# Windowed attention with a feed-forward block: 256-token groups of all heads, a row maximum, and transposes by DMA

## The chip, the cores and the metric

The kernel runs on one core of a Trainium2 chip. A core has five engines, each with its own queue of instructions: PE (matrix multiplication), DVE (vector work), ACT (activation functions), POOL (general work, and the issue of transfers that cast) and SP (which here only issues transfers). Sixteen DMA engines move the data. The metric is the device time of one execution in microseconds.

## The reference

Four batches of eight heads, 768 tokens, 64 elements a head. Each query sees the 128 keys up to itself and the first four keys (the sinks). The heads are put side by side, 3072 tokens by 512, and go through a feed-forward block with a gate of the form h * sigmoid(1.702 h).

```python
scores = scale * np.matmul(q, k.transpose(0, 1, 3, 2))
keep = (pos[None, :] < n_sink) | ((rel >= 0) & (rel < window))
scores = np.where(keep, scores, -1000000000.0)
scores = scores - np.max(scores, axis=-1, keepdims=True)
a = np.exp(scores)
a = a / (np.sum(a, axis=-1, keepdims=True) + 1e-09)
x = np.matmul(a, v)                      # heads side by side: 3072 x 512
h = x @ w_in                             # 512 x 2048
out = (h * (1.0 / (1.0 + np.exp(-1.702 * h)))) @ w_out
```

## The kernel before

The attention works in 16 units of one batch and one pair of heads (768 tokens). For a unit, POOL issues loads that cast q, k and v from 32 to 16 bits straight into SBUF (`loads_qk`, `loads_v`, L129 to L143); each is cut into rows of 64 elements. `t_chunk` (L156 to L158) transposes q and k on PE against an identity matrix and DVE copies the result out of PSUM. `s_chunk` (L174) computes scores transposed, keys on the partitions and queries along the row, for the key blocks that a query can see; the first key block takes all 768 queries, for the sinks. ACT takes the exponential (L183), with no maximum subtracted, and `mask_chunk` multiplies two rows of 1920 columns by a 0/1 mask on DVE (L191). `av_chunk` (L207) multiplies with v, which carries a column of ones, so that the 65th column is the sum; DVE takes the reciprocal and normalises (L214, L215). `xt_chunk` (L227, L229) transposes the result on PE into xT.

The feed-forward block works in eight pieces of 384 tokens. `f_chunk` (L241) makes one of 16 hidden blocks: four matmuls, a tanh on ACT (L246), and a product on DVE (L247). `mm2_chunk` (L257) sums 16 matmuls into one bank of 128 tokens by 512, which ACT copies (L264) and SP stores (L265).

The loop over 16 units writes the order of PE's work out by hand: up to eight hidden blocks and two output blocks, taken from two lists as they become ready, stand between the score, transpose and value chunks of the neighbouring units. After the last unit, hidden and output blocks alternate. PSUM is shared out as four banks for scores and outputs, two for hidden blocks and two for transposes and values.

## Time and profile before

| | |
|---|---|
| runs, median (lowest to highest) | 262.49 us (261.63 to 263.02) |
| profiled execution, span from first to last instruction | 260.1 us |
| mean granted clock of PE | 0.998 |
| PE busy | 238.2 us |
| DVE busy | 158.6 us |
| ACT busy | 138.4 us |
| POOL busy | 74.3 us |
| DMA packets | 81607, 20.76 MB |
| of them in casting loads (q0) | 77696, 13.64 MB |
| HBM read, written | 27.79 MB, 6.29 MB |

The page gives the profiled execution by its span alone; the runs' times are taken around the whole launch. Busy shares are means over stages that differ: the first fifth of the span loads and computes attention, the middle mixes attention with the feed-forward block, the last quarter is feed-forward only. Idle time of an engine costs something only where another engine waits for it, so the rows that matter are those of the chain that ends last. PE's matmuls are pipelined: the distance between the starts of two is their price, not the duration of one.

### The profile page before, as it was taken

The numbers are of one execution on the slowest core, as the hardware profiler recorded it, in microseconds if no ns is written. First come the engines' busy times: TensorE is split into PE (matmuls) and PEld (weight loads), VectorE is DVE, ScalarE is ACT, GpSimd is POOL, SyncE is SP. The second block draws the span as 40 slices with busy tenths as digits, with TensorE's granted clock in tenths as the row PEclk, the third lists the DMA queues.
The fourth block names the chain that finished last, engine by engine and source line by source line (L and its number), as shares of the span: only waits on it lengthen the run. The fifth ranks groups of instructions, "written<-read, shape, count | busy, mean of one in ns | idle before, by whom it ended". The sixth has DMA issues, their size and how long they took to land.

```text
span 260.1 us, 4792 instructions
## 1 busy us (share of the span) xinstructions
PE 238.2 (92%) x1888; PEld 131.4 (51%) x1888; DVE 158.6 (61%) x320; ACT 138.4 (53%) x282; POOL 74.3 (29%) x92
## 2 busy tenths in 40 slices
PE   0749787999999999999999999999999999999993
PEld 0415444565646464555546464555545555555541
DVE  4337989898958685495918684493915833543300
ACT  1257666868438483757538483757533633644311
POOL 8977788773535151133310100000000000000000
PEclk9999999999999999999999999999999999999999
DMA  9999999999959393595960140101021011111112
GB/s 137 139 175 182 176 173 175 179 174 136 92 73 117 20 115 20 106 63 73 61 79 35 8 65 22 59 3 40 4 79 44 0 42 40 43 40 40 40 43 81
DMA packets 81607, 20.76 MB, mean 80 GB/s; under 512 B 75697, under 2 KB 78001, under 8 KB 81585
## 3 DMA queue, kind: packets, MB, share of 16 engines
q0 software_dynamic: 77696, 13.64, 66.1%
q1 hardware_dynamic: 3888, 6.82, 7.1%
q8 instruction: 15, 0.25, 0.4%
q14 instruction: 8, 0.06, 0.1%
HBM read 27.79 MB, written 6.29 MB: 131 GB/s over the span
## 4 chain that ended last, share of the span: by engine, by line
PE 82%; ACT 5%; DVE 4%; POOL 3%; DMA 3%; issue 1%; ACTq 0%; POOLq 0%
DMA qn_2_126<-in_q_dram 3%; PE o_1_2_3359 L257 1%; PE o_1_1_3339 L257 1%; PE o_1_0_3319 L257 1%; PE o_0_2_3267 L257 1%; PE o_0_1_3215 L257 1%; PE o_0_0_3163 L257 1%; PE o_1_2_3079 L257 1%; PE o_1_1_3027 L257 1%; PE o_1_0_2975 L257 1%; PE o_0_2_2809 L257 1%; PE o_0_1_2771 L257 1%; PE o_1_2_2584 L257 1%; PE o_1_1_2395 L257 1%; PE o_0_1_1985 L257 1%; PE o_0_0_1965 L257 1%
## 5 line engine op out<-in xcount | busy, mean ns | idle before, releaser
L241 PEld LDWEIGHTS <-w_in_77 128*128 128x128 f16 x512 | 47.8, 98 | 31.4 <-issue 1.1
L257 PEld LDWEIGHTS <-gT_1_90 128*128 128x128 f16 x48 | 4.7, 98 | 5.5
L257 PEld LDWEIGHTS <-gT_0_89 128*128 128x128 f16 x48 | 4.7, 98 | 5.3
L257 PEld LDWEIGHTS <-gT_0_87 128*128 128x128 f16 x48 | 4.7, 98 | 5.3
L257 PEld LDWEIGHTS <-gT_1_88 128*128 128x128 f16 x48 | 4.7, 98 | 5.3
L257 PEld LDWEIGHTS <-gT_1_84 128*128 128x128 f16 x48 | 4.7, 98 | 5.2
L257 PEld LDWEIGHTS <-gT_0_85 128*128 128x128 f16 x48 | 4.7, 98 | 5.2
L257 PEld LDWEIGHTS <-gT_1_86 128*128 128x128 f16 x48 | 4.7, 98 | 5.2
L156 PE MATMUL tqku_0_108<-ident_73,qn_0_91 128*128 128x128 f16 x2 | 0.6, 288 | 7.1 <-DMA qn_0_91<-in_q_dram 7.1
L257 PEld LDWEIGHTS <-gT_0_83 128*128 128x128 f16 x48 | 4.7, 98 | 4.8
L143 POOL DMA_DIRECT2D v_3_2433<-in_v_dram x1 | 1.0, 1007 | 15.3 <-issue 15.3
L183 ACT ACTIVATE ATu_136<-s0u_0_137 128x512 f16<-128x512 f32 x1 | 0.6, 597 | 7.9 <-PE s0u_1_138 L174 7.9
L156 PEld LDWEIGHTS <-qn_0_91 128*128 128x128 f16 x6 | 0.7, 125 | 7.1 <-issue 7.1
L247 DVE SCALAR_TENSOR_TENSOR gT_0_87<-th_0_6_2420,hT_0_6_2415 128x384 f16<-128x384 f16 x1 | 0.6, 553 | 5.9 <-ACT th_0_6_2420 L246 5.9
L257 PE MATMUL o_0_0_1145<-w_out_78,gT_0_83 128*128 128x512 f16 x16 | 4.1, 379 | 0.0
L247 DVE SCALAR_TENSOR_TENSOR gT_1_88<-th_1_6_2796,hT_1_6_2791 128x384 f16<-128x384 f16 x1 | 0.6, 554 | 5.7 <-ACT th_1_6_2796 L246 5.7
L247 DVE SCALAR_TENSOR_TENSOR gT_0_85<-th_0_6_1600,hT_0_6_1595 128x384 f16<-128x384 f16 x1 | 0.6, 553 | 5.3 <-ACT th_0_6_1600 L246 5.3
L247 DVE SCALAR_TENSOR_TENSOR gT_1_86<-th_1_6_2010,hT_1_6_2005 128x384 f16<-128x384 f16 x1 | 0.6, 553 | 5.3 <-ACT th_1_6_2010 L246 5.3
L257 PE MATMUL o_0_2_1360<-w_out_78,gT_0_83 128*128 128x512 f16 x16 | 3.8, 379 | 0.0
L257 PE MATMUL o_0_0_1965<-w_out_78,gT_0_85 128*128 128x512 f16 x16 | 3.8, 379 | 0.0
L257 PE MATMUL o_1_2_2584<-w_out_78,gT_1_86 128*128 128x512 f16 x16 | 3.8, 379 | 0.0
L257 PE MATMUL o_1_0_2375<-w_out_78,gT_1_86 128*128 128x512 f16 x16 | 3.8, 379 | 0.0
(1546 smaller groups left out, 810.9 us busy)
## 6 DMA issues: line engine op xcount, KB each, us to landing
w_in_77<-in_moe_w_in_dram POOLq DMA_DIRECT2D x4, 512.0 KB, 8.6
w_out_78<-in_moe_w_out_dram POOLq DMA_DIRECT2D x4, 512.0 KB, 8.8
maskall<-cmask SPq DMA_DIRECT2D x1, 480.0 KB, 3.9
out_dram<-osb_0_0_1146 SPq DMA_DIRECT2D x1, 256.0 KB, 2.1
out_dram<-osb_0_1_1166 SPq DMA_DIRECT2D x1, 256.0 KB, 3.6
out_dram<-osb_0_2_1361 SPq DMA_DIRECT2D x1, 256.0 KB, 3.6
out_dram<-osb_1_0_1556 SPq DMA_DIRECT2D x1, 256.0 KB, 3.7
out_dram<-osb_1_1_1576 SPq DMA_DIRECT2D x1, 256.0 KB, 2.3
```

What stands on the lines that cost most here:

```text
L143: nc.gpsimd.dma_start(v65[:, :, :, 0:D], v[b, h0 : h0 + 2].rearrange("h (i s) d -> s h i d", s=P))
L156: nc.tensor.transpose(tp[:, 0, i], qn[:, I], ident16)
L183: nc.scalar.activation(out=AT[:, hl, c0 : c0 + col], in_=st[hl][:, 0:col], func=AF.Exp, scale=scale,)
L241: nc.tensor.matmul(hT, w_in16[:, c, bass.ts(F, P)], xT[c][:, tok0 : tok0 + TT], start=(c == 0), stop=(c == 3),)
L247: nc.vector.scalar_tensor_tensor(out=gT[b, j][:, F], in0=th, scalar=1.0, in1=hT, op0=ALU.add, op1=ALU.mult)
L257: nc.tensor.matmul(ops, gT[b, j][:, F, bass.ts(t4, P)], w_out16[:, F], start=(F == 0), stop=(F == NF - 1),)
```

## The change

The kernel is written anew around groups of 256 tokens of one batch and all eight heads; there are 12. The order of every engine is the order of the program text.

- q and k are cast into DRAM (`load_qk`) and come from there transposed by DMA (`transposed_qk`). The exponentials, the sink weights and the normalised result are transposed by DMA from SBUF to SBUF (L238, L250, L300). All transposes are issued by SP.
- Scores have queries on the partitions. A query block sees its own key block and the one before; of the two, each column is needed from exactly one, so a predicated copy on DVE puts both into one tile of 128 columns (`maxima`). DVE then takes the row maximum, and its minimum form with the sinks' becomes the bias of the exponential (`weights`). After the transpose, the tile is parted again: a select on POOL (`up`) and a mask product on DVE (`lo`) (`parts`).
- Sinks are computed apart (`sinks`, `sink_weights`), as 64 columns for all heads, and enter the value product through a table `vs` of their values.
- The hidden block covers 256 tokens, two blocks to a bank, and the gate is one activation from PSUM to the 16-bit gT (`hidden`). `out_part` makes an output block in four parts; ACT copies and stores it.
- Iteration n of the loop holds the attention of group n, the hidden blocks of group n - 1 and the output blocks of group n - 2. The first two score tiles of group n + 1 are made at its end.
- PSUM: two score tiles of two banks each, two hidden banks, one value bank (shared with the sinks), one output bank.

```diff
+TG = 256
+BIG = 1.0e9
+def _take_prev(first: bool) -> np.ndarray:
+    q, c = np.arange(P)[:, None], np.arange(P)[None, :]
+    m = np.broadcast_to((c > q)[:, None, None, :], (P, 2, 2, P)).copy()
+    if first:
+        m[:, :, 0] = ((c > q) & (c >= 4))[:, None]
+    return m.astype(np.uint16).reshape(P, 4 * P)
+def _own(first: bool) -> np.ndarray:
+    c, q = np.arange(P)[:, None], np.arange(P)[None, :]
+    m = np.broadcast_to((c <= q)[:, None, None, :], (P, 2, 2, P)).copy()
+    if first:
+        m[:, :, 0] = True
+    return m.astype(np.float16).reshape(P, 4 * P)
+def _sink_off(n_sink: int) -> np.ndarray:
+    q, j = np.arange(P)[:, None], np.arange(n_sink)[None, :]
+    m = np.zeros((P, 4, 2, 2, n_sink), np.float32)
+    m[:, :, 0] = BIG
+    m[:, :, 1] = np.where(q >= j, 0.0, BIG)[:, None, None, :]
+    return m.reshape(P, 16 * n_sink)
...
+    ctx.enter_context(tc.manual_schedule())
...
+    q16 = [[dram.tile([TG, DM], FP16, name=f"q16_{b}_{t}") for t in range(NT)] for b in range(B)]
+    k16 = [[dram.tile([TG, DM], FP16, name=f"k16_{b}_{t}") for t in range(NT)] for b in range(B)]
...
+    def load_qk(g: int):
+        b, t = divmod(g, NT)
+        for src, dst in ((q, q16), (k, k16)):
+            nc.gpsimd.dma_start(
+                dst[b][t].rearrange("s (h d) -> s h d", h=H),
+                src[b, :, bass.ts(t, TG)].rearrange("h s d -> s h d"),
+            )
...
-    def t_chunk(u: int):
...
-    def s_chunk(u: int, part: int):
...
-    def mask_chunk(u: int):
...
-    def av_chunk(u: int, g: int):
...
-    def xt_chunk(u: int, g: int):
...
-    def f_chunk(b: int, j: int, F: int, nth: int):
...
-    def mm2_chunk(b: int, j: int, t4: int, nsplit: int = 1):
...
+    def transposed_qk(g: int):
+        b, t = divmod(g, NT)
+        if t == 0:
+            KT[b] = work.tile([P, HP, S], FP16, tag="kT", bufs=2, name=f"kT{b}")
+        nc.sync.dma_start_transpose(KT[b][:, :, bass.ts(t, TG)], k16[b][t])
+        qT = work.tile([P, HP, TG], FP16, tag="qT", bufs=3, name=f"qT{g}")
+        nc.sync.dma_start_transpose(qT, q16[b][t])
+        G[g]["qT"] = qT
+    def sink_keys(b: int):
+        for h in range(2):
+            nc.gpsimd.tensor_copy(
+                out=kd[b][bass.ts(h, D), :, bass.ts(h, n_sink)],
+                in_=KT[b][bass.ts(h, D), :, 0:n_sink],
+            )
...
+    def sinks(g: int):
+        b, t = divmod(g, NT)
+        qT = G[g]["qT"]
+        sk = psp.tile([P, HP, 2, 2 * n_sink], FP32, tag="av", bufs=1, name=f"sk{g}")
+        for hp in range(HP):
+            for i in range(2):
+                nc.tensor.matmul(sk[:, hp, i], qT[:, hp, bass.ts(i, P)], kd[b][:, hp], start=True, stop=True)
+        sn = work.tile([P, 16, n_sink], FP32, tag="sn", name=f"sn{g}")
...
+            nc.vector.tensor_scalar(out=flat, in0=skf, scalar1=-scale, scalar2=None, op0=ALU.mult)
+        m2 = work.tile([P, 16], FP32, tag="m2", name=f"m2{g}")
+        nc.vector.tensor_reduce(out=m2, in_=sn, axis=AX.X, op=ALU.min)
+        G[g].update(sn=sn, m2=m2, bias=work.tile([P, 16], FP32, tag="bias", name=f"bias{g}"))
+    def scores(g: int, hp: int):
+        b, t = divmod(g, NT)
+        qT, kT = G[g]["qT"], KT[b]
+        nat = psp.tile([P, 2, 2, 2 * P], FP32, tag="nat", bufs=2, name=f"nat{g}_{hp}")
+        for i in range(2):
+            I = 2 * t + i
+            if I == 0:
+                for h in range(2):
+                    r = bass.ts(h, D)
+                    nc.tensor.matmul(nat[:, h, i, 0:P], masked_l[r], masked_r[r], start=True, stop=True)
+            for h in range(2):
+                r = bass.ts(h, D)
+                lo = max(I - 1, 0) * P
+                o = nat[:, h, i, P:] if I == 0 else nat[:, h, i]
+                nc.tensor.matmul(
+                    o, qT[r, hp, bass.ts(i, P)], kT[r, hp, lo : (I + 1) * P], start=True, stop=True
+                )
+        G[g]["nat", hp] = nat
+    def maxima(g: int, hp: int):
+        t = g % NT
+        natf = G[g]["nat", hp].rearrange("p h i c -> p (h i) c")
+        nc.vector.copy_predicated(
+            out=natf[:, :, P:], mask=take_prev[t == 0].rearrange("p (a c) -> p a c", a=4), data=natf[:, :, 0:P]
+        )
+        m1 = work.tile([P, 2, 2], FP32, tag="m1", name=f"m1{g}_{hp}")
+        nc.vector.tensor_reduce(
+            out=m1.rearrange("p h i -> p (h i)"), in_=natf[:, :, P:], axis=AX.X, op=ALU.max
+        )
+        nc.vector.scalar_tensor_tensor(
+            out=G[g]["bias"][:, bass.ts(hp, 4)].rearrange("p (i h) -> p i h", i=2),
+            in0=m1.rearrange("p h i -> p i h"),
+            scalar=-scale,
+            in1=G[g]["m2"][:, bass.ts(hp, 4)].rearrange("p (i h) -> p i h", i=2),
+            op0=ALU.mult,
+            op1=ALU.min,
+        )
+    def weights(g: int, hp: int):
+        nat, bias = G[g]["nat", hp], G[g]["bias"]
+        A = work.tile([P, 4, P], FP16, tag="A", bufs=3, name=f"A{g}_{hp}")
+        for h in range(2):
+            for i in range(2):
+                c = 4 * hp + 2 * i + h
+                nc.scalar.activation(
+                    out=A[:, 2 * h + i], in_=nat[:, h, i, P:], func=AF.Exp, bias=bias[:, c : c + 1], scale=scale
+                )
+        AT = work.tile([P, 4, P], FP16, tag="AT", bufs=4, name=f"AT{g}_{hp}")
+        nc.sync.dma_start_transpose(AT, A.rearrange("p a c -> p (a c)"))
+        G[g]["AT", hp] = AT
+    def sink_weights(g: int):
+        sn, bias = G[g]["sn"], G[g]["bias"]
+        ts_ = work.tile([P, 16, n_sink], FP32, tag="ts", name=f"ts{g}")
+        nc.vector.tensor_tensor(
+            out=ts_, in0=bias.unsqueeze(2).broadcast_to((P, 16, n_sink)), in1=sn, op=ALU.subtract
+        )
+        As = sinkA[g % 2]
+        nc.scalar.activation(out=As[:, 0:64], in_=ts_.rearrange("p a j -> p (a j)"), func=AF.Exp)
+        AsT = work.tile([P, 1, P], FP16, tag="AsT", bufs=2, name=f"AsT{g}")
+        nc.sync.dma_start_transpose(AsT, As)
+        G[g]["AsT"] = AsT
+    def parts(g: int, hp: int):
+        t = g % NT
+        AT = G[g]["AT", hp]
+        lo = work.tile([P, 4, P], FP16, tag="lo", bufs=3, name=f"lo{g}_{hp}")
+        up = work.tile([P, 4, P], FP16, tag="up", bufs=3, name=f"up{g}_{hp}")
+        nc.gpsimd.affine_select(
+            out=up, in_=AT, pattern=[[0, 4], [-1, P]], compare_op=ALU.is_gt, fill=zero_reg, base=0,
+            channel_multiplier=1,
+        )
+        nc.vector.tensor_tensor(
+            out=lo.rearrange("p a c -> p (a c)"), in0=AT.rearrange("p a c -> p (a c)"), in1=own[t == 0], op=ALU.mult
+        )
+        G[g]["lo", hp], G[g]["up", hp] = lo, up
+    def values(g: int, hp: int):
+        b, t = divmod(g, NT)
+        lo, up, AsT = G[g]["lo", hp], G[g]["up", hp], G[g]["AsT"]
+        av = psp.tile([P, 2, 2, D + 1], FP32, tag="av", bufs=1, name=f"av{g}_{hp}")
+        for i in range(2):
+            I = 2 * t + i
+            if I > 0:
+                nc.tensor.matmul(
+                    av[:, i].rearrange("p h d -> p (h d)"), AsT[:, 0],
+                    vs[b][:, 4 * hp + 2 * i : 4 * hp + 2 * i + 2].rearrange("p h d -> p (h d)"),
+                    start=True, stop=False,
+                )
+            for h in range(2):
+                head = 2 * hp + h
+                if I > 0:
+                    J = I - 1
+                    nc.tensor.matmul(
+                        av[:, i, h], up[:, 2 * h + i], vn[b][J // 2][:, J % 2, head], start=False, stop=False
+                    )
+                nc.tensor.matmul(
+                    av[:, i, h], lo[:, 2 * h + i], vn[b][t][:, i, head], start=(I == 0), stop=(I == 0 or h == 1)
+                )
+        if hp == 0:
+            G[g]["xn"] = work.tile([P, 2, HP, 2, D], FP16, tag="xn", name=f"xn{g}")
+        rcp = work.tile([P, 2, 2], FP32, tag="rcp", name=f"rcp{g}_{hp}")
+        nc.vector.reciprocal(out=rcp, in_=av[:, :, :, D])
+        nc.vector.tensor_tensor(
+            out=G[g]["xn"][:, :, hp], in0=av[:, :, :, 0:D], in1=rcp.to_broadcast((P, 2, 2, D)), op=ALU.mult
+        )
+    def x_transposed(g: int):
+        xT = work.tile([P, 2 * HP, P], FP16, tag="xT", bufs=3, name=f"xT{g}")
+        nc.sync.dma_start_transpose(xT, G[g]["xn"].rearrange("p i a h d -> p (i a h d)"))
+        G[g]["xT"] = xT.rearrange("p (i c) s -> p i c s", i=2)
+    def hidden(g: int, F2: int):
+        xT = G[g]["xT"]
+        if F2 == 0:
+            G[g]["gT"] = work.tile([P, NF, TG], FP16, tag="gT", name=f"gT{g}")
+        hT = psp.tile([P, 2, 2, P], FP32, tag="hT", bufs=2, name=f"hT{g}_{F2}")
+        for f in range(2):
+            F = 2 * F2 + f
+            for c in range(4):
+                nc.tensor.matmul(
+                    hT[:, f], w_in16[:, c, bass.ts(F, P)], xT[:, :, c], start=(c == 0), stop=(c == 3)
+                )
+        nc.scalar.activation(
+            out=G[g]["gT"][:, 2 * F2 : 2 * F2 + 2].rearrange("p f s -> p (f s)"),
+            in_=hT.rearrange("p f i s -> p (f i s)"),
+            func=AF.Gelu_apprx_sigmoid,
+        )
+    def out_part(g: int, i: int, part: int):
+        b, t = divmod(g, NT)
+        if part == 0:
+            G[g]["o", i] = psp.tile([P, DM], FP32, tag="o", bufs=1, name=f"o{g}_{i}")
+        o, gT = G[g]["o", i], G[g]["gT"]
+        for F in range(4 * part, 4 * part + 4):
+            nc.tensor.matmul(o, gT[:, F, bass.ts(i, P)], w_out16[:, F], start=(F == 0), stop=(F == NF - 1))
+        if part == 3:
+            osb = work.tile([P, DM], FP32, tag="osb", bufs=3, name=f"osb{g}_{i}")
+            nc.scalar.copy(osb, o)
+            r = b * S + t * TG + i * P
+            nc.scalar.dma_start(out[r : r + P, :], osb)
...
+    transposed_qk(0)
+    sink_keys(0)
+    load_v(1)
+    load_w_in(1)
+    load_w_in(2)
+    load_w_in(3)
+    sink_values(0)
+    load_qk(2)
+    load_v(2)
+    load_w_out(0)
+    load_w_out(1)
+    load_w_out(2)
+    load_w_out(3)
+    def ahead(n: int):
+        if n < NG:
+            sinks(n)
+            for hp in (0, 1):
+                scores(n, hp)
+                maxima(n, hp)
+    ahead(0)
+    for n in range(NG + 2):
+        att = n < NG
+        g1, g2 = n - 1, n - 2
+        if n + 1 < NG:
+            transposed_qk(n + 1)
+            if (n + 1) % NT == 0:
+                sink_keys((n + 1) // NT)
+        if att:
+            weights(n, 0)
+        if 0 <= g2:
+            out_part(g2, 0, 0)
+            out_part(g2, 0, 1)
+        if att:
+            weights(n, 1)
+            scores(n, 2)
+            maxima(n, 2)
+            weights(n, 2)
+        if 0 <= g2:
+            out_part(g2, 0, 2)
+            out_part(g2, 0, 3)
+        if att:
+            scores(n, 3)
+            maxima(n, 3)
+        if 0 <= g2:
+            out_part(g2, 1, 0)
+        if att:
+            weights(n, 3)
+            sink_weights(n)
+            parts(n, 0)
+        if 0 <= g2:
+            out_part(g2, 1, 1)
+            out_part(g2, 1, 2)
+            out_part(g2, 1, 3)
+        if n + 3 < NG:
+            load_qk(n + 3)
+            load_v(n + 3)
+        if n + 1 < NG and (n + 1) % NT == 0:
+            sink_values((n + 1) // NT)
+        if n == 0:
+            ahead(1)
+        f1 = 0 <= g1 < NG
+        for F2 in range(NF // 2):
+            if f1:
+                hidden(g1, F2)
+            if att and F2 in (0, 1, 2):
+                parts(n, F2 + 1)
+            if att and F2 in (2, 3, 4, 5):
+                values(n, F2 - 2)
+            if F2 == 5 and n > 0:
+                if n + 1 < NG:
+                    sinks(n + 1)
+                    scores(n + 1, 0)
+                    maxima(n + 1, 0)
+            if F2 == 6 and n > 0 and n + 1 < NG:
+                scores(n + 1, 1)
+                maxima(n + 1, 1)
+        if att:
+            x_transposed(n)
```

## The prediction

> **What bounds the kernel now.** I read the page's busy shares and slices first, then the chain in order of time, then stretches, then single rows for prices.
>
> ```profile
> span 260.1 us, 4792 instructions
> PE 238.2 (92%) x1888; PEld 131.4 (51%) x1888; DVE 158.6 (61%) x320; ACT 138.4 (53%) x282; POOL 74.3 (29%) x92
> PE   0749787999999999999999999999999999999993
> ACT  1257666868438483757538483757533633644311
> DMA  9999999999959393595960140101021011111112
> ```
>
> PE is full from slice 8 on; the DMA engines are full only before that. The chain says the same: loads in the first 20 us, then PE line after PE line to the end.
>
> ```profile
> 11.02 7.15 DMA qn_2_126<-in_q_dram
> ...
> 80.90 0.66 PE avu_1_1279 L207 x18
> 81.56 0.65 PE hT_1_8_1302 L241 x4
> 82.21 0.17 PE xtu_0_1310 L227 x3
> ...
> 93.69 0.10 PE s3u_0_1466 L174
> ...
> 102.23 3.45 PE o_1_1_1575 L257 x16
> 249.29 3.45 PE o_1_1_3339 L257 x16
> ```
>
> Seen here: 0.163 us a hidden matmul of 384 columns, 0.216 an output matmul of 512, 0.037 a value matmul of 65, 0.055 a 128-column transpose, and 0.11 a pair of 256-column scores (0.10 here, s3u_1 runs beside s3u_0). The stretches show where PE waits and where not:
>
> ```profile
> 0.00:47.00 47.00, 30.56 (x326) 18.39 (x327) 31.60 (x63) 24.84 (x50) 38.94 (x51) 1.00 1.76 166
> 75.00:190.00 115.00, 113.90 (x927) 62.34 (x926) 75.86 (x155) 68.36 (x140) 19.79 (x23) 1.00 0.48 53
> ```
>
> Columns: length, PE, weight loads, DVE, ACT, POOL, granted clock (1.00), DMA share, GB/s. ACT has 47 us of slack in the second stretch, so ACT's waits cost nothing now.
>
> Prices for the other engines, from the timeline and the DMA issues:
>
> ```profile
> 0.73 1.28 ACT L183 ACT_TABLE_LOAD   x1 [0.73 <-PEq L368]
> 7.77 0.27 PE L157 MATMUL tqku_0_108<-ident_73,kn_0_92 128*128 128x128 f16 x1 [0.26 <-DMA kn_0_92<-in_k_dram]
> 20.22 0.59 POOL L103 DMA_DIRECT2D w_in_77<-in_moe_w_in_dram  x1
> 26.50 0.59 POOL L103 DMA_DIRECT2D w_in_77<-in_moe_w_in_dram  x1
> 102.89 0.33 SPq L265 DMA_DIRECT2D out_dram<-osb_1_0_1556  x1
> 108.01 0.42 DVE L158 COPY qkTu_1637<-tqku_0_1638 128x512 f16<-128x512 f16 x1
> 109.86 0.20 DVE L214 RECIPROCAL rcpu_0_1658<-avu_0_1656 128x6 f32<-128x6 f32 x1 [0.27 <-PE avu_0_1656 L207]
> 110.09 0.56 DVE L215 TENSOR_TENSOR xnu_0_1657<-avu_0_1656,rcpu_0_1658 128x384 f16<-128x384 f32 x1
> 110.68 0.59 ACT L183 ACTIVATE ATu_1622<-s3u_1_1682 128x512 f16<-128x512 f32 x1
> 256.29 0.66 ACT L264 ACTIVATE osb_1_2_3360<-o_1_2_3359 128x256 f32<-128x256 f32 x2 [2.91 <-PE o_1_2_3359 L257]
> ...
> out_dram<-osb_0_0_2752 SPq DMA_DIRECT2D x1, 256.0 KB, 2.0
> qn_3_636<-in_q_dram POOLq DMA_DIRECT2D x2, 96.0 KB, 7.8
> ```
>
> **The change: PE work.** Before: 512 x 0.163 + 384 x 0.216 = 166 us, plus per head pair 12 x 0.055 + 0.82 (3840 score columns, two heads side by side, at 0.11 per 512) + 30 x 0.037 + 6 x 0.055 = 2.9, x16 = 47; 213 in all. After: hidden 768 x 0.109 (two thirds of 0.163) = 84, output 83, and per group scores 4 x 0.22, sinks 8 x 0.037, values 4 x 0.41 = 2.8, x12 = 34; 200. The transposes leave PE: 13 us less. One full iteration is 6.9 output + 7.0 hidden + 2.8 = 16.7 us.
>
> **Where it waits.** Ten iterations (n = 2 to 11) are full. The program now has 21 table loads on the way, 27 us at 1.28, since Exp and the gate alternate; it had one. I walk one iteration from the moment PE ends the last hidden pair. ACT's prices: 128 columns cost 0.19 each in a row (the eight ACTIVATEs of a unit, 3840 columns, run from 107.40 to 111.27, 0.84 ns a column) to 0.27 alone (0.59 less 384 x 0.84 ns); I take 0.25, as a per-partition bias has no row, so 1.05 for the four of a head pair. The gate and a copy, both 128x512: 0.6. DVE: 0.20 fixed and 0.96 ns a column (0.56 at 384) give 0.70 for 512; predicated copy 0.70, maximum 0.70, small row 0.20 = 1.65 for one `maxima` with handovers. Both large ones have no row: 0.42 (the plain copy) to 0.75; I take 0.70, nearest to two-operand work on PSUM.
>
> - ACT: last gate to 0.65, table load to 1.95, weights 0 to 3.0, weights 1 to 4.05. PE: output parts to 1.72, then `scores(n,2)` needs the bank that weights 0 frees: 1.4 us idle, done at 3.3; parts to 5.0, `scores(n,3)` to 5.25.
> - DVE: maxima 2 to 5.05; ACT: weights 2 to 6.15, copy of the output bank to 6.75. That bank exists once, so the second output block starts at 6.85: 1.6 us idle; PE ends it at 10.3. Weights 3 and sink weights finish at 8.4 beside it.
> - ACT: copy to 10.95, the store's issue 0.33 (it moves from SP to ACT, so the table load queues behind it), table load to 12.6, gate to 13.2. PE has two hidden banks, so the third pair waits from 12.05 to 13.25: 1.2 us. Then hidden and values to 18.4; `sinks(n+1)` shares the one value bank and waits 0.7 for DVE; end 21.6.
>
> So 16.7 + 4.9 = 21.6 us. With the short prices (exponentials 0.19, DVE 0.42) the same walk gives 20. DVE's other work (lo 4 x 0.34, normalisation 4 x 0.65) totals 11 us and lies beside PE.
>
> The Trainium skill, "ScalarE: Activation LUTs", What ACT_TABLE_LOAD costs, states about 2.66 us for a switch including a drain, and its rule to batch calls by table set speaks against this change. The trace's one load took 1.28, at a moment with nothing to drain. By the page's figure both loads on the way grow by 1.4 and the walk gives 24.4 (an estimate), 28 us more in all.
>
> **Transposes by DMA.** No row. Below: the 256 KB store, 2.0 us to landing; above: a load of 768 short rows on full queues, 7.8. I take 3.5, nearer the store, which like these is one SP issue. At 3.5 the weights of the last head pair (8.15) and the sinks are in by 12.4, before values at 14.1: hidden. At 7.8 they come at about 16.3, and an iteration is 2.2 longer. The last transpose of an iteration (x) is issued at about 19 and needed 10 us into the next one. SP is one queue: the k and q transposes of group n+1 wait there for their loads, and behind them stand all weight transposes of group n. If those loads were late, values, normalisation and the next hidden block would be late by the same amount; their cover is that loads run three groups ahead.
>
> **Loads.** Steps of 6.28 us (20.22 to 26.50) carried 4608 rows and a 512 KB weight part. A group of 6144 rows is therefore at most 8.4 us; two thirds of the rows now go to DRAM and back, unpriced: from no more to double, 14 us. Either is under 20 and hidden once started. POOL's queue counts too: each group's four issues (about 1.2 + 1.2 + 0.9 + 0.9, from 0.82 for 768 rows and 1.03 for 1536) stand between its first and second select. A select has no POOL row; 0.3 (mask multiply rate) to 1.0 (its longest issue), I take 1.0; covered.
>
> **The start.** q and k of group 0: the first 3072 rows were in at 7.77; 4096 rows, about 9.5. Transposes 13, scores 15, weights of group 0 from 15.6 to 21.9. POOL copies the sink keys at 13.5, when kT is there, and behind them issues v (2 x 0.9), three w_in (0.6), the sink values (no row, taken as 2), q and k (2 x 1.2), v, four w_out (0.8): 26.5. After the first select, group 3's four loads wait for group 2's to land (bytes at the rate of the 6.28 us steps: about 29) and end at 31.8; three more selects 34.8. So values of group 0 end at 36 and x is transposed at 39.5, where the first hidden block begins. Iteration 1's second select stands behind loads that wait for w_out, in at about 40; with 7.0 of hidden and 1.6 of values between, it ends at 50. Bounds: 42 if POOL is never late, 63 if three transposes in series take 7.8. PE had done 30.6 us of work by 47 before; here it will have done about 12.
>
> **The end.** Iteration 12: output 6.9 + 0.7, hidden 7.0; then gate 0.65, output 7.6, copy and store 3: 26.
>
> **Sum.** 50 + 10 x 21.6 + 26 = 292 us of span. The page gives the profiled execution's span, 260.1; the runs (261.63 to 263.02, median 262.49) stand 1.5 to 2.9 above it. I add 2.4 for what lies around the span, as the median does: 294.
>
> **Rivals.** (a) Faster: PE stays the bound because ACT's table loads fall under output matmuls. Speaking for it: 13 us less PE work, 47 us of ACT slack in a 115 us stretch. Against: the single output bank and the two score banks tie PE to ACT's order. At 17.5 an iteration and a start of 45: 45 + 175 + 26 + 2.4 = 248. It decides below 18.4 an iteration (at a start of 50). (b) Slow transposes: 7.8 us each, 63 + 10 x 23.8 + 26 + 2.4 = 329; DMA at 0.48 share in the steady stretch speaks against queues being that full. (c) The loads through DRAM double: the start grows by about 5 and nothing else, 299; inside the forecast's range.
>
> **How the numbers follow.** Forecast with (c), 272 to 315: 0.60. Rival (a), under 261.2: 0.12. Within 0.5% of 262.5 (about what a measurement tells from no change): 0.03. Between that and 272: 0.05. Rival (b), 315 to 338: 0.13; beyond, if transposes and loads are slow together: 0.07. The range 260 to 338 leaves out most of (a) and the last 0.07. The forecast's own range is 272 to 315.
>
> **What would show it.** PE's busy share near 70%, ACT_TABLE_LOAD x22; PE idle before L203 on ACT L234 (1.4), before L328 on ACT L331 (1.6), before L312 on ACT L315 (1.2); iterations about 21.6 apart by the stores; transposes landing in 3 to 4 us. Wrong if iterations are under 18.4, or if PE waits on DMA for AT or kT in the steady part.

## The result and the profile after

The changed kernel takes 377.96 us in the median (374.37 to 380.04, four runs) against 262.51 us for the kernel before in the same session: a ratio of 1.432, 95% interval 1.422 to 1.442. The ratio leaves out the execution of 380.04 us, which was in the chip's slower state; the two medians by themselves give 1.440. The forecast was 294.0 us with a range of 260 to 338. The direction was right, the size was not. The profiled execution has a span of 372.2 us and took 374.37 us.

The page of the changed kernel, busy shares and slices:

```profile
span 372.2 us, 5170 instructions
PE 229.4 (62%) x1904; PEld 145.7 (39%) x1904; DVE 140.1 (38%) x352; ACT 152.7 (41%) x346; POOL 100.7 (27%) x120
PE   0010211367767767667667677587587877878995
...
PEclk9999999999989989989989989989989999999999
DMA  9997999995987975945927955924915163321101
```

No engine is full. PE has little to do before 74 us. From there to about 280 us PE stays near 0.7, DMA comes in bursts near 0.9, and PEclk loses a tenth once in about three slices, which is once an iteration. Only at the end, when no loads are left, PE rises to 0.8.

An iteration can be cut at ACT's table load for Exp. These come at 89.38, 116.65, 143.28, 171.02, 198.64, 225.28, 252.59, 280.27, 302.70 and 325.59 us. The first seven distances, during which the loads of later groups run, have a mean of 27.27 us; the last two are 22.43 and 22.89 us. Two stretches of the changed kernel, cut in this way (columns: length, busy time with counts for PE, weight loads, DVE, ACT, POOL, then granted clock, DMA share, GB/s), one with loads and one without. The DMA share of a stretch sums the times of all packets that start in it over 16 engines, and as packets overlap it can pass 1.

```profile
198.64:225.28 26.64, 18.80 (x154) 11.97 (x152) 10.99 (x28) 12.90 (x29) 7.18 (x8) 0.94 1.00 96
...
302.70:325.59 22.89, 17.92 (x162) 11.26 (x160) 10.69 (x28) 12.90 (x29) 2.94 (x4) 1.00 0.44 74
```

ACT does the same 12.90 us in both. What differs is the DMA share, 1.00 against 0.44, and the granted clock, 0.94 against 1.00.

PE's rows of the first of these iterations, in order of time (A holds the exponentials, AT their transpose, AsT that of the sink weights); the bracket is the idle time before a row and what ended it:

```profile
201.13 0.23 PE L198 MATMUL nat<-maskedr,maskedl 64*128 64x128 f16 x2 [1.40 <-ACT A L234]
...
205.00 3.61 PE L328 MATMUL o<-w_out,gT 128*128 128x512 f16 x16 [1.32 <-ACT osb L331]
...
211.58 1.03 PE L312 MATMUL hT<-xT,w_in 128*128 128x256 f16 x8 [1.22 <-ACT gT L315]
...
215.75 0.29 PE L275 MATMUL av<-vs,AsT 128*128 128x130 f16 x1 [3.07 <-DMA AsT<-sinkA]
...
216.07 1.90 PE L312 MATMUL hT<-xT,w_in 128*128 128x256 f16 x8
...
218.21 1.26 PE L312 MATMUL hT<-xT,w_in 128*128 128x256 f16 x8
...
221.69 0.34 PE L175 MATMUL sk<-kd,qT 128*128 128x8 f16 x8 [0.83 <-DVE xn L294]
```

And of the one without loads:

```profile
309.06 3.61 PE L328 MATMUL o<-w_out,gT 128*128 128x512 f16 x16 [1.32 <-ACT osb L331]
...
315.64 1.03 PE L312 MATMUL hT<-xT,w_in 128*128 128x256 f16 x8 [1.22 <-ACT gT L315]
316.51 0.22 PE L275 MATMUL av<-vs,AsT 128*128 128x130 f16 x1
```

The waits for ACT and DVE (1.40, 1.32, 1.22, 0.83 us) are the same in both; the prediction's walk had 1.4, 1.6, 1.2 and 0.7. New is the fourth row of the first fence: 3.07 us for the transposed sink weights AsT. The rows behind it are slower as well: eight hidden matmuls take 1.90 and 1.26 us where 1.03 is usual. Wait and slower matmuls together are 4.2 us. That is the whole difference between this iteration, 26.64 us, and the one without loads that also holds the first group of a batch, 22.43 us (280.27 to 302.70). Over the seven iterations PE waits 22.9 us for AsT, 3.3 us each.

Why AsT is late can be read from the two queues that issue transfers. SP in the same iteration:

```profile
201.14 6.86 SPq L238 DMA_TRANSPOSE AT<-A  x4
208.10 1.18 SPq L250 DMA_TRANSPOSE AsT<-sinkA  x1
```

and POOL:

```profile
203.58 0.63 POOL L259 TENSOR_SCALAR_AFFINE_SELECT up<-AT 128x512 f16<-128x512 f16 x1 [13.16 <-DMA AT<-A]
204.16 1.23 POOL L114 DMA_DIRECT2D q<-in_q_dram  x1
205.26 1.40 POOL L114 DMA_DIRECT2D k<-in_k_dram  x1
206.28 2.14 POOL L122 DMA_DIRECT2D vn<-in_v_dram  x2
```

The first weight transpose is issued at 201.14 and its reader starts at 203.58: at most 2.44 us to landing. Behind that reader POOL issues the four loads of group n + 3. AsT, issued at 208.10 into those loads, is used at 215.75: 7.65 us, and 7.6 to 8.1 in all seven. In the three iterations without loads it was in use 4.3 to 4.4 us after its issue, with no wait for it.

The start, from PE's rows:

```profile
20.18 0.37 PE L175 MATMUL sk<-kd,qT 128*128 128x8 f16 x8 [20.18 <-DMA qT<-q]
...
36.48 0.29 PE L198 MATMUL nat<-maskedr,maskedl 64*128 64x128 f16 x2 [14.96 <-ACT A L234]
...
50.80 0.29 PE L275 MATMUL av<-vs,AsT 128*128 128x130 f16 x1 [8.25 <-DMA AsT<-sinkA]
...
65.93 3.57 PE L312 MATMUL hT<-xT,w_in 128*128 128x256 f16 x16 [8.15 <-DMA xT<-xn]
75.07 1.86 PE L312 MATMUL hT<-xT,w_in 128*128 128x256 f16 x8 [5.57 <-ACT gT L315]
```

and ACT's:

```profile
3.64 31.55 ACTq L349 DMA_DIRECT2D vsr<-in_v_dram  x16
35.29 2.18 ACT L234 ACTIVATE A<-nat,bias 128x128 f16<-128x128 f32 x8 [30.40 <-DMA vsr<-in_v_dram]
```

Sixteen small loads of the sinks' values, issued by ACT, keep ACT's queue from 3.64 to 35.2 us, so that the first exponentials come at 35.3 us; then the transposes of the sink weights and of x take 7.8 and 8.4 us each from issue to use, one after the other. Iteration 2 starts at 89.4 us.

### The profile page after: what moved, and what is told of

Read it like the earlier page. It is cut to its first block, busy times and chain, and to the rows that moved or that the text cites. A ratio compares the mean times of both kernels' runs of the same rounds, so it can differ in the third digit from the quotient of the medians.

```text
span 372.2 us, 5170 instructions
## 1 busy us (share of the span) xinstructions
PE 229.4 (62%) x1904; PEld 145.7 (39%) x1904; DVE 140.1 (38%) x352; ACT 152.7 (41%) x346; POOL 100.7 (27%) x120
## 3 DMA queue, kind: packets, MB, share of 16 engines
q0 software_dynamic: 78720, 13.64, 48.7%
## 5 line engine op out<-in xcount | busy, mean ns | idle before, releaser
L312 PE MATMUL hT<-xT,w_in 128*128 128x256 f16 x768 | 107.2, 291 | 25.9 <-ACT gT L315 17.8
L328 PE MATMUL o<-w_out,gT 128*128 128x512 f16 x384 | 88.5, 379 | 14.6 <-ACT osb L331 14.6
L315 ACT ACTIVATE gT<-hT 128x512 f16<-128x512 f32 x96 | 56.1, 596 | 100.0 <-PE hT L312 99.7
L312 PEld LDWEIGHTS <-w_in 128*128 128x128 f16 x768 | 75.9, 104 | 46.2 <-issue 32.2
L259 POOL TENSOR_SCALAR_AFFINE_SELECT up<-AT 128x512 f16<-128x512 f16 x48 | 38.0, 827 | 184.3 <-DMA AT<-A 132.0
L234 ACT ACTIVATE A<-nat,bias 128x128 f16<-128x128 f32 x192 | 53.7, 375 | 77.2 <-DMA vsr<-in_v_dram 30.4
L263 DVE TENSOR_TENSOR lo<-AT,own 128x512 f16<-128x512 f16 x48 | 26.8, 579 | 105.2 <-PE av L287 60.4
L328 PEld LDWEIGHTS <-gT 128*128 128x128 f16 x384 | 36.6, 97 | 56.7 <-issue 18.9
L211 DVE COPY_PREDICATED nat<-prev,nat 128x512 f32<-128x512 uint16 x48 | 33.4, 695 | 45.0 <-PE nat L203 44.9
L275 PE MATMUL av<-vs,AsT 128*128 128x130 f16 x80 | 19.2, 251 | 34.0 <-DMA AsT<-sinkA 33.6
L215 DVE TENSOR_REDUCE m<-nat 128x4 f32<-128x512 f32 x48 | 33.2, 691 | 1.6
L175 PE MATMUL sk<-kd,qT 128*128 128x8 f16 x96 | 4.2, 167 | 28.5 <-DMA qT<-q 20.2
L114 POOL DMA_DIRECT2D k<-in_k_dram x12 | 17.4, 1446 | 0.3 <-DMA k<-in_k_dram 0.3
```

Of the source, the lines that this page charges most:

```text
L211: nc.vector.copy_predicated(out=natf[:, :, P:], mask=take_prev[t == 0].rearrange("p (a c) -> p a c", a=4), data=natf[:, :, 0:P])
L215: nc.vector.tensor_reduce(out=m1.rearrange("p h i -> p (h i)"), in_=natf[:, :, P:], axis=AX.X, op=ALU.max)
L234: nc.scalar.activation(out=A[:, 2 * h + i], in_=nat[:, h, i, P:], func=AF.Exp, bias=bias[:, c : c + 1], scale=scale)
L259: nc.gpsimd.affine_select(out=up, in_=AT, pattern=[[0, 4], [-1, P]], compare_op=ALU.is_gt, fill=zero_reg, base=0, channel_multiplier=1,)
L263: nc.vector.tensor_tensor(out=lo.rearrange("p a c -> p (a c)"), in0=AT.rearrange("p a c -> p (a c)"), in1=own[t == 0], op=ALU.mult)
L275: nc.tensor.matmul(av[:, i].rearrange("p h d -> p (h d)"), AsT[:, 0], vs[b][:, 4 * hp + 2 * i : 4 * hp + 2 * i + 2].rearrange("p h d -> p ...
```

## Experiments

Beside every run the kernel before was timed again; it stood between 262.1 and 262.7 us, and the ratios below are to it. Gains in us are differences of medians; starts and lengths of iterations are read from the one execution that was profiled. Several runs start from the third one, the late loads, instead of from the changed kernel.

### Which term is it: four single edits of the changed kernel

**The small sink loads left out**

```diff
-                nc.scalar.dma_start(vsr[r : r + 4], v[:, 2 * hp + h, 0:n_sink].rearrange("b j d -> j b d"))
+    nc.vector.memset(vsr, 0.0)
```

> The sixteen small loads of the sink rows of v on ACT's queue are left out (the sink rows are set to zero, so the sinks' share of the values is left out). Theory 'ACT's queue is held': the first exponentials start when their bias is ready, near 23 us instead of 35.3, and the whole gains about 12 us (8 to 14): near 366. Rival 'the loads set the start anyway' (q, k, v and the weights on POOL's queue): the first exponentials come early but iteration 2 still starts near 88; gain under 4 us: 374 to 378.

Measured: 371.92 us, 6.0 less (ratio to before 1.419, 1.413 to 1.425). The first exponentials do start at 23.9 us, as the theory says, but iteration 2 starts at 83.3, 6.1 us earlier instead of 12. SP's rows of this run show where the other half went:

```profile
21.62 6.75 SPq L149 DMA_TRANSPOSE qT<-q  x1
28.47 11.42 SPq L238 DMA_TRANSPOSE AT<-A  x4
39.98 1.18 SPq L250 DMA_TRANSPOSE AsT<-sinkA  x1
```

The weights are ready at 25 us, but SP holds the transpose of group 1's q in front of them until 28.4, and the four of A take 11.4 us to issue. Neither theory had the size; the hold on ACT is real and here worth about 6 us.

**No loads for groups 3 to 11**

```diff
-    q16 = [[dram.tile([TG, DM], FP16, name=f"q16_{b}_{t}") for t in range(NT)] for b in range(B)]
+    q16 = [[dram.tile([TG, DM], FP16, name=f"q16_{t}") for t in range(NT)]] * B
...
-        if n + 3 < NG:
-            load_qk(n + 3)
-            load_v(n + 3)
```

> The loads of q, k and v for groups 3 to 11 are left out; their work is done on the rows of groups 0 to 2 (so the outputs of those groups are of other data). All transposes, matmuls and stores stay. Theory 'casting loads beside the DMA transposes': every iteration takes the 22.9 us that iterations 9 to 11 took, seven of them 4.4 less, so -31 us or a little more (near 345), and PE no longer waits for the sinks' transpose. Rival 'the transposes delay each other': iterations stay at 27.3, gain under 5 us.

Measured: 333.61 us, 44.4 less (1.275, 1.270 to 1.281). All iterations now take 22.4 to 23.0 us, and iteration 2 starts at 79.5 instead of 89.4: seven times 4.5 (27.27 less 22.76) plus 9.9 is 41.4, which is the change of the span, 372.2 to 330.8. The gain is larger than expected because the start gains too. The loads are the cause of the long iterations; that transposes delay each other is out.

**The same loads at the end of the iteration**

```diff
-        if n + 3 < NG:
-            load_qk(n + 3)
-            load_v(n + 3)
         if n + 1 < NG and (n + 1) % NT == 0:
             sink_values((n + 1) // NT)
...
+        if n + 3 < NG:
+            load_qk(n + 3)
+            load_v(n + 3)
         if att:
             x_transposed(n)
```

> The same loads, but each group's four are issued at the end of an iteration's work on POOL, after its last mask, not before its second. Theory 'when they meet': the loads then land beside the output matmuls, away from the weight transposes, iterations near 23, so -20 to -30 us (348 to 358). Rival 'how much is moved' (the same traffic slows whatever transposes it meets, x's and the next weights'): within 5 us of 378, the wait of PE only at another place.

Measured: 341.09 us, 36.9 less (1.302, 1.298 to 1.305), more than the expected 20 to 30. Iteration 2 starts at 89.0, so nothing of it is the start. The profiled spans differ by 31.8 us (372.2 and 340.4), seven times the 4.5 us by which an iteration got shorter; the rest is that the fastest execution of the changed kernel was profiled and the slowest of this one. A stretch of this kernel, the counterpart of 198.64 to 225.28 above:

```profile
180.19:202.62 22.43, 17.46 (x154) 10.91 (x152) 11.43 (x28) 12.90 (x29) 7.35 (x8) 1.00 0.97 116
```

and PE's rows in a later iteration:

```profile
262.28 0.22 PE L275 MATMUL av<-vs,AsT 128*128 128x130 f16 x1
...
262.46 1.04 PE L312 MATMUL hT<-xT,w_in 128*128 128x256 f16 x8
```

The DMA share is 0.97, as high as before the move, with PE's wait gone and the granted clock at 1.00. So it is not how much is moved in an iteration, but that the loads were in the queues when the weights had to be transposed.

**One table**

```diff
-            func=AF.Gelu_apprx_sigmoid,
+            func=AF.Tanh,
```

> The gate is Tanh, which shares a table with Exp (so the gate's values are others). Theory 'table loads on the way': two of 1.28 us go from each of ten iterations, -22 to -27 us (351 to 356). Rival 'only one is on the way, or the transposes set the time': -5 to -13 us in all. By the Trainium skill's 2.66 us for a switch it would be about -53 us.

Measured: 361.01 us, 17.0 less (1.378, 1.373 to 1.383). Between the numbers of theory and rival, and the iterations say why: the last two without loads fall to 19.7 and 20.2 us, by the full two table loads, while those with loads stay between 25.7 and 27.0 us. PE's wait for AsT takes up what ACT saves: 3.9 to 5.4 us in place of 3.0 to 3.6.

### The same terms with the loads out of the way

**One table on top of the late loads**

> On top of the late loads (341.1): Tanh as the gate (other values). With the loads early this gave -17 us. Theory 'the transposes ate the rest': with that wait gone, both loads of 1.28 us come off each of the ten iterations in full, -24 to -27 us: 314 to 317, an iteration 20.2 instead of 22.75. Rival 'only some of it is on the path': -17 again, 324.

Measured: 319.65 us, 21.4 less than the late loads (1.215, 1.205 to 1.224). The nine iterations have a mean of 20.66 us, 2.1 less than 22.75; the theory wanted 2.56. The table loads were hidden by the wait, as the theory said. They do not come off quite in full: behind the start PE still waits for AsT six times, 3.9 us in all. In these six AsT is used 2.3 to 2.4 us after its issue, so this is the transpose by itself, which PE now reaches sooner, and not the loads.

**No row maximum on top of the late loads**

```diff
-        nc.vector.tensor_reduce(
-            out=m1.rearrange("p h i -> p (h i)"), in_=natf[:, :, P:], axis=AX.X, op=ALU.max
-        )
...
-        G[g].update(sn=sn, m2=m2, bias=work.tile([P, 16], FP32, tag="bias", name=f"bias{g}"))
+        G[g].update(sn=sn, bias=zero_bias)
```

> On top of the late loads (341.1): no row maximum, the bias is a tile of zeros; the predicated copy stays. Theory 'the maximum lies on the path only through the second score block': the exponentials of head pair 2 no longer wait for DVE (0.85 us of reduce and small row), the copy of the output bank and all behind it come about 0.9 us earlier in each of ten iterations: -8 to -12 us, 329 to 333. Rival 'DVE is off the path, ACT's own order sets it': under 4 us.

Measured: 330.86 us, 10.2 less (1.260, 1.251 to 1.269). The iterations have a mean of 21.8 us, 1.0 less than 22.75. With the loads late, the row maximum is worth 10 us; what it costs beside the early loads was not run.

**The copy of the output bank first**

```diff
             maxima(n, 2)
-            weights(n, 2)
         if 0 <= g2:
             out_part(g2, 0, 2)
             out_part(g2, 0, 3)
         if att:
+            weights(n, 2)
             scores(n, 3)
```

> On top of the late loads (341.1): the four exponentials of head pair 2 are put behind the copy of the first output bank on ACT. Theory 'PE waits 1.32 us for the bank because ACT does exponentials first': the copy starts as the bank is full, 1.0 us earlier in each of ten iterations: -8 to -11 us, 330 to 333. Rival 'the weights of head pair 2 are then late': their transposes and values later by 1 us, the wait comes back before the values, under 3 us.

Measured: 333.23 us, 7.9 less (1.264, 1.254 to 1.273); the iterations have a mean of 22.05 us, 0.7 less. The order of two pieces of work on ACT is worth nearly as much as the row maximum.

**The last two together**

> Late loads, no row maximum and the copy first, with the gate of the changed kernel (two table loads an iteration). Alone on top of the late loads the second gave 10.2 us, the third 7.9. Theory 'separate': 320 to 326. Rival 'the same wait': the wait for the output bank can go only once, 329 to 333.

Measured: 329.92 us (1.257, 1.248 to 1.267): no less than without the maximum alone. The rival holds: both edits shorten the one wait for the output bank, which is 1.32 us before and 0.35 after either.

**All four edits, with Tanh and a DVE product as the gate**

```diff
-            func=AF.Gelu_apprx_sigmoid,
+        nc.scalar.activation(out=th, in_=hf, func=AF.Tanh, scale=0.851)
+        nc.vector.scalar_tensor_tensor(
+            out=G[g]["gT"][:, 2 * F2 : 2 * F2 + 2].rearrange("p f s -> p (f s)"),
+            in0=th, scalar=1.0, in1=hf, op0=ALU.add, op1=ALU.mult,
+        )
...
-            nc.scalar.copy(osb, o)
+            nc.scalar.mul(osb, o, 0.5)
```

> Late loads, no row maximum, the copy first, and the gate as Tanh and a DVE product (one table), together. One by one the runs gave 36.9, 10.2, 7.9 and 21.5 us. Theory 'separate terms of one chain': 378 less most of their sum, 300 to 310, an iteration 18 to 19.5 us. Rival 'they share one wait, or the DVE product takes its place': 312 or more. Neither gives less than 262.5, since the start stays near 85 us and the tail at 26.

Measured: four runs from 334.2 to 344.0 us. Even the lowest is 33 us above what the single gains add up to (36.9, 21.4, 10.2 and 7.9 off 377.96 leave 301.6). In the execution that was profiled (340.2 us, not the lowest) PE waits 0.7 us for the product in every iteration (hT waits for DVE's gT), and values wait 0.7 to 1.2 us for DVE's normalisation, which queues behind the products of 0.69 us each.

**The four edits without the product**

> The four edits without the DVE product (Tanh is then the whole gate, its values are others; late loads, no row maximum, copy first stay). Theory 'the product on DVE cost what the table loads gave': without it the terms add up, 300 to 308, an iteration near 19 us, granted clock 0.98 or more. Rival 'the terms overlap, or PE is granted less clock as it gets fuller': 318 or more, an iteration still above 20.5 us, clock under 0.97.

Measured: 321.94 us (1.221, 1.210 to 1.233). Without the product 12 us come off the lowest of the four, but that is no less than one table on the late loads alone (319.65). The rival holds in its time and its iterations, which take 19.2 to 25.2 us, 21.2 in the mean; the granted clock was 0.968 in the profiled execution, but 0.984 to 0.993 in the other three. PE's rows in the longest iteration, then SP's and one of ACT's:

```profile
160.68 1.03 PE L298 MATMUL hT<-xT,w_in 128*128 128x256 f16 x8 [2.48 <-ACT gT L301]
162.71 0.29 PE L261 MATMUL av<-vs,AsT 128*128 128x130 f16 x1 [0.99 <-DMA AsT<-sinkA]
...
163.35 1.90 PE L298 MATMUL hT<-xT,w_in 128*128 128x256 f16 x8
...
165.72 1.90 PE L298 MATMUL hT<-xT,w_in 128*128 128x256 f16 x8
```

```profile
146.52 4.26 SPq L147 DMA_TRANSPOSE kT<-k  x1
...
152.54 7.68 SPq L224 DMA_TRANSPOSE AT<-A  x4
160.33 1.17 SPq L236 DMA_TRANSPOSE AsT<-sinkA  x1
```

```profile
157.82 1.14 ACT L220 ACTIVATE A<-nat,zerobias 128x128 f16<-128x128 f32 x4 [3.42 <-DMA AT<-A]
```

As the iteration gets shorter, the transposes of A come back into the loads: here they are issued from 152.54, behind that of k, which holds SP for 4.26 us. ACT waits 3.42 us until one of them frees a tile of A for its last exponentials, and PE waits for the gate that stands behind these on ACT. AsT itself takes 2.38 us from issue to use, and 2.3 to 2.4 in all these iterations: it is not slow, it is issued late. After the 3.5 us of waiting two hidden groups take 1.90 us each. The terms are not separate: behind the work taken off ACT and DVE stand the transposes.

### What in the loads holds the transposes

**Only v loaded, at the early place**

```diff
         if n + 3 < NG:
-            load_qk(n + 3)
             load_v(n + 3)
```

> The changed kernel with its loads at their early place, but for groups 3 to 11 only v is loaded; q and k are those of groups 0 to 2 (other data). Theory 'by amount': v is a third of what is fetched, so a third of the 44 us that all the loads cost stays: 345 to 352. Rival 'the detour of q and k through DRAM': nearly all of it goes with them: 333 to 339. Rival 'any casting load among the transposes': at least half stays: 356 or more.

Measured: 341.79 us, 36.2 less (1.301, 1.296 to 1.307), between the numbers of the first theory and of the detour. The iterations have a mean of 23.0 us against 22.76 with no loads at all: v alone, at the same place, costs them next to nothing. Most of the 8 us left over no loads at all lies in the start (iteration 2 at 86.3 instead of 79.5).

**q and k fetched to SBUF, where nobody reads them**

```diff
+        for src, dst in zip((q, k), aside):
+            for i in range(2):
+                nc.gpsimd.dma_start(
+                    dst[:, i], src[b, :, t * TG + i * P : t * TG + (i + 1) * P].rearrange("h s d -> s h d")
+                )
```

> As the run that loads only v for groups 3 to 11 (341.8; iterations of 23.0 us), but q and k of those groups are fetched too, at the early place, into SBUF tiles that nobody reads, with v's access pattern (two loads each of 128 KB in place of one of 256 KB; the work is done on the q and k of groups 0 to 2). Theory 'the detour: q and k are written to DRAM': the iterations stay near 23, 340 to 348. Rival 'by amount: three loads outlast the weight transposes, one does not': iterations near 27 as in the changed kernel, 370 or more.

Measured: 371.72 us (1.421, 1.410 to 1.431), iterations of 26.9 us in the mean while loads run. The casting queue of this run, then of the run with v alone (packets, MB, share):

```profile
q0 software_dynamic: 79008, 13.64, 53.4%
```

```profile
q0 software_dynamic: 41568, 8.92, 30.3%
```

It is the amount, not the detour through DRAM: with as many packets as the changed kernel has (78720), none of the extra ones written to DRAM, PE waits for AsT again (2.42 and 2.73 us in two iterations) and nearly all of the time comes back. It is no matter of shares either, since a third of the loads cost next to nothing: by these runs and the late loads, what counts is whether the loads are still in the queues when the transposes come. Whether loads of this amount without a cast would hold them as long was not run.

### The start

**Group 1's q and k transposed behind group 0's weights**

```diff
-        if n + 1 < NG:
+        if 0 < n and n + 1 < NG:
             transposed_qk(n + 1)
...
             sink_weights(n)
+            if n == 0:
+                transposed_qk(1)
```

> On top of the late loads (341.1): the small sink loads left out as in the run without them (the sinks' share of the values is left out), and the transposes of group 1's k and q put behind group 0's weight transposes on SP. Theory 'SP's one queue took over the hold from ACT's': the weights of group 0 are transposed from 25 us on (they waited to 28.5 behind group 1's q), and the start gains the 7 us of the run without the small loads and 3 to 5 more: 329 to 334. Rival 'what the transposes meet in the DMA engines sets it': no more than the 7 us: 334 to 341, the transposes of A landing later instead.

Measured: 342.10 us (1.301, 1.292 to 1.311), nothing gained over the late loads, though the sink loads are out too, and above the range of the rival as well. The weights of group 0 are transposed from 25.2 us on, as planned. But k's and q's transposes, now issued at 37.9 and 41.2 us, fall into the weights' loads, and PE waits for them until 56.2 us. Iteration 2 starts at 89.9 us, where it was.

**No weights loaded**

```diff
-    load_w_in(0)
+    nc.vector.memset(w_in16, 0.0)
```

(and so for the other seven parts of the weights)

> On top of the late loads (341.1): w_in and w_out are not loaded but set to zero by DVE in its idle time, so the hidden layer and all outputs are zero. Theory 'the 8 MB of weights are what the start's transposes meet': the sinks' transpose of group 0 (7.9 us) and x's (8.2 us) fall to 3 us each, the loads of group 2 come sooner, and iteration 2 starts at 62 to 72 instead of 89: 314 to 324. Rival 'ACT's queue and the loads of q, k and v set the start': iteration 2 still after 80, gain under 9 us.

Measured: 323.93 us in the median of two runs, 17.2 less than the late loads (1.232, 1.218 to 1.246). Iteration 2 starts at 71.6 us, 17.4 earlier. Time and start are in the theory's ranges, but not for its reason: the transposes of the sink weights and x still take 7.5 and 6.5 us to use (7.9 and 8.2 with the weights), as the loads of groups 2 and 3 are beside them. What went first is the hold on ACT:

```profile
3.64 20.64 ACTq L349 DMA_DIRECT2D vsr<-in_v_dram  x16
24.39 2.18 ACT L234 ACTIVATE A<-nat,bias 128x128 f16<-128x128 f32 x8 [19.50 <-DMA vsr<-in_v_dram]
```

With the weights' loads the sixteen small loads held ACT for 32.4 us in the late-loads run, and the first exponentials came at 36.1. So 11.7 of the 17.4 us are already there at the first exponentials.

**A quiet start**

> Left out together: the loads of groups 3 to 11 (their work is done on the rows of groups 0 to 2), the loads of w_in and w_out (zeros) and the small sink loads (zeros). The loads of groups 0 to 2 stay. Theory 'all of the late start is DMA': iteration 2 starts at 50 to 58 (89.4 in the changed kernel, 71.6 without the weights alone), the transposes of group 0's x and sinks land in under 4 us, and the time is 294 to 303. Rival 'the chain of group 0 and 1 has that length by itself': iteration 2 not before 65, 310 or more.

Measured: 315.72 us (1.202, 1.195 to 1.210). Iteration 2 starts at 62.0 us, between theory and rival, and the expected time was summed with too short an iteration (with nine of 22.75, one of 20.2, the tail of 26.4 and 2.2 around the span, starts of 50 to 58 give 304 to 312, and 62.0 gives 315.6). PE's rows, with the loads of groups 0 to 2 alone:

```profile
33.84 0.29 PE L275 MATMUL av<-vs,AsT 128*128 128x130 f16 x1 [2.78 <-DMA AsT<-sinkA]
...
43.19 3.57 PE L312 MATMUL hT<-xT,w_in 128*128 128x256 f16 x16 [3.47 <-DMA xT<-xn]
50.87 1.87 PE L312 MATMUL hT<-xT,w_in 128*128 128x256 f16 x8 [4.11 <-ACT gT L315]
```

The transposes of AsT (issued at 31.5) and x (39.5) are used after 2.4 and 3.7 us, not 7.8 and 8.4. What is left is the chain of two groups, with their own loads and those of group 2 still in it.

### One part of the change alone, in the kernel before

```diff
-        nc.scalar.activation(out=th, in_=hT, func=AF.Tanh, scale=0.851)
-        nc.vector.scalar_tensor_tensor(
-            out=gT[b, j][:, F], in0=th, scalar=1.0, in1=hT, op0=ALU.add, op1=ALU.mult
-        )
+        nc.scalar.activation(out=gT[b, j][:, F], in_=hT, func=AF.Gelu_apprx_sigmoid)
```

> One part of the change alone, in the kernel before: the gate as one activation in place of Tanh and a DVE product (the factor 0.5 goes too). Theory: Exp and the gate then alternate in its finely interleaved order, each switch is a table load of 1.28 us on ACT, and ACT, 138 us busy, becomes the bound: slower by 10 to 40 us or more, by the number of loads. Rival: DVE loses its product, ACT has slack, the time stays within 3 us of 262.5.

Measured: 275.05 us against 262.07 (1.047, 1.038 to 1.057): slower by 13 us. ACT's groups of this run:

```profile
L183 ACT ACT_TABLE_LOAD x15 | 19.2, 1283 | 1.0 <-PEq L364 0.7
L245 ACT ACT_TABLE_LOAD x15 | 19.2, 1283 | 0.3
```

Thirty table loads, 38.4 us on ACT, and a third of that reaches the end; the theory holds at the lower end of its range. That is the price in this kernel's order of work; in the changed kernel one table instead of two gave 17.0 us, and 21.4 with the loads late.

## Why the prediction was right or wrong

**PE is no longer the bound: right.** PE is busy 62% of the span, 22 table loads are there, and each named wait is at its line with its size: 1.40 (1.4), 1.32 (1.6), 1.22 (1.2), 0.83 (0.7).

**Prices: right.** From the page of the changed kernel (busy us, mean ns):

```profile
L234 ACT ACTIVATE A<-nat,bias 128x128 f16<-128x128 f32 x192 | 53.7, 375 | 77.2 <-DMA vsr<-in_v_dram 30.4
...
L211 DVE COPY_PREDICATED nat<-prev,nat 128x512 f32<-128x512 uint16 x48 | 33.4, 695 | 45.0 <-PE nat L203 44.9
...
L215 DVE TENSOR_REDUCE m<-nat 128x4 f32<-128x512 f32 x48 | 33.2, 691 | 1.6
```

The predicated copy and the maximum were taken at 0.70 us each. Four exponentials take 1.14 us as a group, against 1.05. The gate is 0.60 and a table load 1.28, as taken. Two small things were off: the mask product `lo`, taken at 0.34, has a mean of 0.58, and the 0.84 ns a column is about the step between rows of 384 and of 512 columns, not 3.87 us over 3840 columns, which would be 1.01. Neither shows in a wait of PE.

**The iteration, 21.6 us: short by about 1.** Without the collision it is 22.43 us, and 22.89 for a batch's later groups, whose values include the sinks in both halves. Small differences all along the walk, none of them a missing wait.

**The switch of tables.** The Trainium skill, "ScalarE: Activation LUTs", What ACT_TABLE_LOAD costs, was weighed at 2.66 us a switch, which would have made the iteration 24.4. In this trace the load begins as the activation before it ends and the next begins as the load ends: 1.28 us, no drain beside it. Without the two table loads an iteration fell by 2.1 us. The rule to batch by table held: one table gave 21.4 us on the late loads.

**The transposes, 3.5 us and hidden: this step failed.** By itself one of A or of the sink weights is used 2.3 to 2.4 us after its issue, sooner than was taken (the larger one of x 3.7). Beside the loads AsT takes 7.6 to 8.1 in the steady part, the upper bound of 7.8, and PE waits 3.0 to 3.6 us for it where the prediction had no wait. The prediction put that bound aside because the DMA share of the old steady stretch was 0.48, an average over a stretch of another kernel. In the changed one it is 1.00 in the mean of an iteration and 2.14 in the 4 us in which AsT is under way. And even at 7.8 the iteration was given only 2.2 us more. It got 4.5 (27.27 less the 22.75 of the late loads): 3.3 of waiting, and about 1.2 of slower matmuls behind it, since the wait also takes the clock down. The Trainium skill, "DMA: Bandwidth & Descriptors", Queues, rings and completion order, says that a DMA engine takes packets from its queue rows in turn; that agrees with a transpose which waits its share behind the loads' packets, though no run here shows the order within an engine.

**The loads, "hidden once started": wrong in what was asked.** They were priced by when they land (within 20 us), and they do land in time, 6.5 to 9.5 us after their issue: no iteration of the steady part waits for k or q. They were not priced by what they do to others that share the DMA engines. The rule that loads run three groups ahead covers their own lateness, not that.

**The start, 50 us with bounds 42 to 63: wrong, 89.4.** Three things were missed. The sixteen small loads on ACT's queue were not counted at all (first exponentials at 35.3, not 15.6; at 23.9 without them). The transposes of sink weights, x, k and q stand in series beside the loads of the weights and of groups 2 and 3. Without the weights the start is 17.4 us shorter: 11.7 of that is the small loads' hold, 2.2 the transposes of sink weights and x, and 3.4 a shorter wait for the first gates (4.30 instead of 7.70). Without the rest of the hold and the later groups' loads it is 9.6 us shorter again (71.6 to 62.0). These parts don't add up from single edits: without the small loads alone only 6.1 us came off, as the transposes then met the weights' loads instead. And the quiet chain itself is 62, not 50, with the loads of group 2 still beside it: exponentials at 20.1 (4.5 later), x in PE's hands at 43.2 (3.7 later), and 4.1 us in which PE waits for a gate that ACT can't reach, since ACT holds group 1's last exponentials for a buffer whose transpose stands on SP behind those of x, k and q.

**The tail, 26 us: right**, 26.4.

**The sum.** Start +39.4, ten iterations 256.4 in place of 216: +40.4, of which seven collisions of 4.5 are 31 and the short walk 9; tail +0.4. Together 80.2, the difference of the spans 372.2 and 292. Most of what is left to the median is that the profiled execution was the fastest of the four (374.37).

**The rivals.** (a), an iteration under 18.4, did not come near. (b), slow transposes at 329, had the mechanism and less than half of its size (35 of 84 us): its start of 63 had the transposes in series, but not the small loads nor the waits behind them, and its 23.8 us iteration not the clock. (c), loads doubled by DRAM, is out for the iterations: fetching q and k to SBUF costs them 26.9 us, nearly as much as the detour's 27.27.

No version tried comes near the kernel before; of those that load everything the best is 319.7 us with another gate, and 329.9 us with the reference's gate but no row maximum. Not tried is a start that loads the weights later and keeps ACT's queue free, with the sinks' values kept.

## What to carry to other kernels

A transfer that "lands in time" is not free: ask which other transfers with a reader right behind them will be in the queues at that moment, and issue bulk loads where no such transfer is due (36.9 us here, by moving three lines). Count every small transfer on the queue of an engine that computes. Where single waits sit in one loop, price an edit on top of the others; here four gains that added up to 76 us gave 34 to 44 together, and 56 without the product that one of them needs.

## What the runs showed of the hardware that was not expected

- A DMA transpose of the sink weights (128 x 128) takes 2.3 to 2.4 us from issue to use when no casting load is in the queues, and 7.6 to 8.1 us beside those of a group; x's (128 x 1024) takes 3.7 and 8.4. One issue on SP is 1.2 us, and up to 6.6 in the start (q's of group 1).
- PE's granted clock falls after waits of 2.4 us and more and stays down for some 3 us. Windows of the changed kernel around the wait for AsT:

```profile
212.00:216.00 4.00, 0.93 (x12) 0.75 (x11) 0.00 (x0) 0.61 (x2) 0.00 (x0) 0.91 2.14 158
216.00:220.00 4.00, 4.00 (x40) 3.23 (x38) 1.76 (x7) 1.09 (x2) 0.89 (x1) 0.67 0.05 3
220.00:224.00 4.00, 3.17 (x41) 2.15 (x39) 2.83 (x8) 1.30 (x3) 0.00 (x0) 1.00 0.53 37
```

  The clock is 0.67 in the stretch after the wait, and back at 1.00 in the next: about 1.1 us lost for 3.07 waited. The Trainium skill, "TensorE: Matmul & The Clock Gate", Part 1, gives about 3.4 us of idling as the window after which the clock is halved; here 3.07 us of idling in one piece, with 1.1 us of matmuls between it and a wait of 1.22 us before, were enough. In the run with q and k fetched to SBUF, waits for AsT of 1.90 and 2.17 us, also behind one of 1.2, left the hidden groups at 1.04 us, and one of 2.42 did not (1.55 and 1.90).
- Sixteen loads of 4 KB each, issued by ACT, held its queue for 31.6 us while the casting loads ran, and for 20.6 us with the weights' loads left out (32.4 with them, in the run that it is compared with).
